# Turning the next group's x by DMA instead of on TensorE, and one attention chunk a unit earlier, in a fused local-attention and FFN kernel

## The chip, the cores and the metric

The kernel runs on one core of one Trainium2 chip. Its time is device microseconds of one execution; the time before is the median of three runs, 606.39 us (605.71, 606.39 and 606.4). One further execution was profiled, and all rows of the trace come from it. TensorE's granted clock was 1.0 throughout.

## The reference

The input x is 1 x 2048 x 640, float32. Two branches read the same layer-normalized x, and their product is added to x:

```python
xn = layernorm(x)
qkv = (xn @ wqkv).reshape(B, S, 3, H, Dh)          # 32 heads of 20
idx = pos[:, None] - (arange(8) * 2)[None, :]      # 8 keys, every second token back
logits = einsum("bhsd,bhswd->bhsw", q, k[idx]) * scale   # masked where idx < 0
s = (softmax(logits) with v[idx]).reshape(B, S, D) @ wo
g = silu(silu(xn @ w1) @ w2)                       # w1 640x1536, w2 1536x640
return x + s * g
```

## The kernel before, in words

**Groups.** The 2048 tokens are worked on in four groups of 512: two halves of the sequence, in each the even and then the odd tokens. A group is T = 4 tiles of 128 partitions by 640 columns. The 640 columns are DC = 5 chunks of 128; the 1536 hidden columns are FC = 12 units of 128.

**Products.** A float32 product is made of three matmuls of type float32r: high part by high part, low by high, high by low. So each operand exists as a high and a low half. For the operand that comes from x, TensorE needs columns on partitions: `split_t` turns one chunk. It makes four 128x128 transposes on TensorE (L619) into one of two PSUM banks named rot, ScalarE copies the bank to the high half TH (L623), and VectorE subtracts to the low half TL (L629). For x, ScalarE also copies the turned chunk back into XIN (L625, the buffer of normalized x), so that the subtraction (L626) reads it from there and the bank is free sooner. The turned chunk of attention's output O goes through the same function with L619, L623 and L629, into the halves OH and OL, which share buffers with TH and TL in alternation. Weights stand in a ring WR of seven tiles. At first use ScalarE (L564) and VectorE or GpSimd (L568) split them and SP stores the halves in DRAM (L573); later uses load both halves with one DMA from GpSimd's queue (L555).

**Stages of a group.** `qkv_phase` makes q, k and v (L886 to L888), ScalarE moves them out of PSUM (L641, L643), SP shifts rows between partitions for the window (L654, and L662 to L666 for the two rows carried from the first half of the sequence), and attention runs on VectorE, with an exp on ScalarE at L700 and some adds on GpSimd. It is not finished when the FFN starts: VectorE works at it beside the FFN's matmuls. `ffn_phase` is a list of steps on TensorE (`plan`):

- w1 unit 0, then `wo_phase`, which applies wo to the attention of the group before. VectorE multiplies the result into the gate tile G (L965); for each of the four tiles SP loads x again into one of three buffers xr (L978), GpSimd adds G to it (L979), and SP stores the output (L981).
- then w1 units and w2 units in the order of `STEPS`. A w1 unit (`up`, L1065 to L1067) is 15 matmuls into one rot bank, after which ScalarE writes silu twice, sh and sf (L1078, L1079), and VectorE their difference sl (L1080). A w2 unit (`down`, L930 and L932) is 24 pairs of matmuls with sh and sl, into the six acc banks.
- behind some w2 units, given by the table `AFTER`, the turn of one chunk of the next group's x. That x was loaded (L1010 is used for the last group) and normalized in XIN at the start of the FFN. In the last group there is no next x; there `AFTER` places the first three chunks of the last attention's output (`o_chunk`).
- at the end ScalarE writes silu of the acc banks into G (L1136).

In the last group the two remaining chunks of O are turned by `o_rest` (L779, then L782 and L783), the first two tiles ahead of the last w1 unit and the other two in the midst of it, after `at` chunks of its five. Then `wo_rest` adds the outputs of the third group, and `wo_last` applies wo to the last group. `first_quarter` holds the start of the program.

**Order.** Each engine runs its instructions in order, and each queue of DMAs starts them in order. All steps are put on a list with an engine, an assumed duration, the keys that they read and write, and a priority. The class `Weave` replays that list in a model of time. The order of TensorE is the order of the program; on the other engines the step that can start soonest goes first, by priority among equals. DMAs have an assumed rate and landing time (`RATE`, `LAND`, `more`), `at` holds a step back to a point in the model's time (`clock[0]` is TensorE's place), `late` delays its reader, and `lock` marks steps of VectorE and GpSimd that exclude one another. Where the model shows a gap on TensorE, `plan` tries other orders. `emit` then writes the instructions in the order found. So an edit of one table can move instructions on all engines.

Of the kernel before, what the change touches and what calls it, by code (L numbers as in the profile page):

```python
# [7 lines left out]

F32 = mybir.dt.float32
F32R = mybir.dt.float32r  # L10
AF = mybir.ActivationFunctionType
OP = mybir.AluOpType
AX = mybir.AxisListType

P = 128
# [36 lines left out]
OUT_IN = 6.0  # L52
CARRY_AT = 8.0
X_SINGLE = (1,2,)
QAT = 48
OAT = 16
STORE_Q = 1, 3
# [257 lines left out]
def local_attention_silu_ffn(ctx: ExitStack, tc: tile.TileContext, x, wqkv, wo, w1, w2, out):  # L315
# [11 lines left out]
    AFTER = ({1: 0, 3: 1, 5: 2, 7: 3, 9: 4}, {1: 0, 3: 1, 5: 2, 7: 3, 9: 4}, {1: 0, 3: 1, 5: 2, 7: 3, 9: 4}, {5: 0, 7: 1, 9: 2})  # L327
    STEPS = [
# [45 lines left out]
    XR = tiles("xr", 3, [P, D])  # L374
    SF = sb.tile([P, TOK], F32, name="sf")
    MARK = small("mark", 1)
    ACC = [psum.tile([P, TOK], F32, name=f"acc{i}") for i in range(6)]
    ROT = [psum.tile([P, TOK], F32, name=f"rot{i}") for i in range(2)]
    carry = [dram.tile([2, NQ, 2, T, CQ], F32, name=f"carry{par}") for par in range(2)]
# [251 lines left out]

    def tile_spans(of, cs, ts):
        return [(of, t * D + c * P, t * D + (c + 1) * P, False) for t in ts for c in cs]
# [417 lines left out]
    def up(g, i, f, io):  # L1054

        wh, wl, kh, kl = w_next("w1", f)
        h, kp = rot()
        s = f % NS

        def first(cs):  # L1060
            to = h.rearrange("p (m h) -> p m h", h=2)
            for c in cs:
                cs = tsl(c)
                hi, lo = (two(v[i][:, c, :], 0, TOK, TOK // 2) for v in (TH, TL))
                nc.tensor.matmul(to, wh[:, cs], hi, start=c == 0, stop=False)  # L1065
                nc.tensor.matmul(to, wh[:, cs], lo, start=False, stop=False)  # L1066
                nc.tensor.matmul(to, wl[:, cs], hi, start=False, stop=c == DC - 1)  # L1067
        at = 2 if g == NG - 1 and f == FC - 1 else DC
        for a, b in ((0, at), (at, DC)):
            if a == b:  # L1070
                continue
            if a:
                o_rest(g, (2, 3), io)
                wo_rest(g - 1, io)
            pe(3 * (b - a) * mm(TOK), lambda a=a, b=b: first(range(a, b)), t_keys(i, range(DC)) + [kh, kl], [kp])
        w_done()
        sh, sl = SH[s], SL[s]
        act(TOK, lambda: nc.scalar.activation(halves_of(sh), paired(h), AF.Silu), [kp], [("sh", s)], 0, "silu")  # L1078
        act(TOK, lambda: nc.scalar.activation(halves_of(SF), paired(h), AF.Silu), [kp], ["sf"], 0, "silu")  # L1079
        dve(TOK, lambda: nc.vector.tensor_tensor(out=sl, in0=SF, in1=sh.bitcast(F32), op=OP.subtract),  # L1080
            [("sh", s), "sf"], [("sl", s)], 0, lock=True)
# [24 lines left out]
    def ffn_phase(g, i, ix, io):  # L1106
        if g + 1 < NG:
# [7 lines left out]
            for t in range(T):  # L1115
                ln_apply(t)
        ps = None
        for kind, f in plan(g):
            if kind == "w1":
                up(g, i, f, io)  # L1120
            elif kind == "wo":
                wo_phase(g - 1, io)
                if g == NG - 1:
                    free_for([("xin", t) for t in range(T)], [("xin", t, c) for t in range(T) for c in (0, CA)])
            elif kind == "x":
                split_t(XIN, [("xin", t) for t in range(T)], f, ix, (TH, TL), XIN[:, :, tsl(f)])
            elif kind == "o":
                o_chunk(g, f, io)
            elif kind == "rest":
                o_rest(g, f, io)  # L1130
# [46 lines left out]
```

## Time and profile before

| | before |
|---|---|
| median of three runs | 606.39 us |
| profiled execution | 605.28 us |
| span in its trace | 603.5 us |
| busiest engine | TensorE, 597.0 us in 3495 matmuls |
| next | VectorE 518.4, ScalarE 222.2, GpSimd 165.7 us |
| bytes moved by DMA | 160.80 MB, 266 GB/s over the span |

Rows of the trace are read as follows. In a timeline and in the chain a row has the start in us from the span's start, the duration in us, the engine, and the source line with the operation; "out<-in" are the program's names of the buffers, then shapes and a count; brackets at the end give the idle time before the row and what ended it. PEld is TensorE's loading of weights, SPq and POOLq are DMAs that SP and GpSimd issue. In the table of groups the columns behind the bar are total busy time (us), mean of one (ns), and the idle time before.

The FFN of the second group lies at about 189 to 286 us of the span, that of the third at 337 to 434 us; the last w1 unit of the fourth group begins at about 571 us.

### The profile page before, as it was taken

The numbers are of one execution on the slowest core, as the hardware profiler recorded it, in microseconds if no ns is written. First come the engines' busy times: TensorE is split into PE (matmuls) and PEld (weight loads), VectorE is DVE, ScalarE is ACT, GpSimd is POOL, SyncE is SP. The second block draws the span as 40 slices with busy tenths as digits, with TensorE's granted clock in tenths as the row PEclk, the third lists the DMA queues.
The fourth block names the chain that finished last, engine by engine and source line by source line (L and its number), as shares of the span: only waits on it lengthen the run. The fifth ranks groups of instructions, "written<-read, shape, count | busy, mean of one in ns | idle before, by whom it ended". The sixth has DMA issues, their size and how long they took to land.

```text
span 603.5 us, 9128 instructions
## 1 busy us (share of the span) xinstructions
PE 597.0 (99%) x3495; PEld 562.0 (93%) x3495; DVE 518.4 (86%) x505; ACT 222.2 (37%) x426; POOL 165.7 (27%) x229
## 2 busy tenths in 40 slices
PE   8999999999999999999999999999999999999997
PEld 7999999999999999999999999999999999999897
DVE  6599999999799969999969999999727999998534
ACT  5447364453436124333324522242512341314220
POOL 5800111233110254343210126433122233531100
PEclk9999999999999999999999999999999999999999
DMA  9999999779999998655699998866789997766642
GB/s 294 308 321 323 330 407 394 285 244 303 284 323 293 320 318 250 205 169 163 185 320 285 328 348 289 273 210 178 226 220 274 301 324 259 249 186 210 209 163 87
DMA packets 66119, 160.80 MB, mean 266 GB/s; under 512 B 5805, under 2 KB 30093, under 8 KB 66077
## 3 DMA queue, kind: packets, MB, share of 16 engines
q0 software_dynamic: 19296, 79.31, 43.4%
q1 hardware_dynamic: 46237, 80.52, 43.0%
q8 instruction: 27, 0.44, 0.3%
q10 hardware_dynamic: 544, 0.41, 0.2%
q14 instruction: 15, 0.12, 0.1%
HBM read 107.91 MB, written 34.16 MB: 235 GB/s over the span
## 4 chain that ended last, share of the span: by engine, by line
PE 98%; DVE 1%; DMA 1%; ACT 0%; issue 0%
PE acc L930 22%; PE acc L932 15%; PE acc L886 10%; PE acc L887 10%; PE acc L888 10%; PE rot L1065 9%; PE rot L1067 9%; PE rot L1066 9%; PE rot L619 2%; PE acc L836 2%; DMA xin<-in_A_x_dram 1%; PE rot L820 0%; PE rot L1048 0%; DVE st L805 0%; DVE tl L629 0%; ACT th L623 0%
## 5 line engine op out<-in xcount | busy, mean ns | idle before, releaser
L680 DVE TENSOR_TENSOR pr<-q,kv 128x2560 f32<-128x2560 f32 x32 | 91.9, 2873 | 22.0 <-DMA kv<-kv 17.6
L886 PE MATMUL acc<-w,th 128*128 128x480 f32 x300 | 110.8, 369 | 0.0
L887 PE MATMUL acc<-w,tl 128*128 128x480 f32 x300 | 109.8, 366 | 0.0
L888 PE MATMUL acc<-w,th 128*128 128x480 f32 x300 | 109.8, 366 | 0.0
L930 PE MATMUL acc<-w,sh 128*128 128x384 f32 x384 | 109.1, 330 | 0.0
L932 PE MATMUL acc<-w,sh 128*128 128x256 f32 x384 | 104.7, 273 | 0.0
L1065 PE MATMUL rot<-th,w 128*128 128x512 f32 x240 | 92.2, 384 | 1.0 <-DVE tl L629 1.0
L722 DVE TENSOR_TENSOR pr<-q,kv 128x2560 f32<-128x2560 f32 x32 | 90.3, 2820 | 0.9
L1066 PE MATMUL rot<-tl,w 128*128 128x512 f32 x240 | 91.0, 379 | 0.0
L1067 PE MATMUL rot<-th,w 128*128 128x512 f32 x240 | 91.0, 379 | 0.0
L683 DVE TENSOR_REDUCE l<-pr 128x128 f32<-128x2560 f32 x32 | 89.6, 2799 | 0.2
L555 POOL DMA_DIRECT2D w<-half_w x72 | 39.0, 542 | 153.8 <-PE rot L1067 51.0
L932 PEld LDWEIGHTS acc<-w,sh 128*128 128x128 f32 x384 | 73.7, 192 | 0.6
L930 PEld LDWEIGHTS acc<-w,sh 128*128 128x128 f32 x384 | 72.6, 189 | 0.6
L1078 ACT ACTIVATE sh<-rot 128x512 fp32r<-128x512 f32 x48 | 28.8, 599 | 113.9 <-PE rot L1067 113.9
L555 POOL DMA_DIRECT2D w<-half_q x52 | 27.9, 537 | 122.6 <-PE acc L888 75.4
L888 PEld LDWEIGHTS acc<-w,th 128*128 128x128 f32 x300 | 56.7, 189 | 4.0
L887 PEld LDWEIGHTS acc<-w,tl 128*128 128x128 f32 x300 | 56.7, 189 | 3.8
L886 PEld LDWEIGHTS acc<-w,th 128*128 128x128 f32 x300 | 56.7, 189 | 3.8
L930 PE MATMUL acc<-w,sl 128*128 128x384 f32 x192 | 55.9, 328 | 0.0
L623 ACT ACTIVATE th<-rot 128x512 fp32r<-128x512 f32 x33 | 19.8, 600 | 89.9 <-PE rot L619 89.9
L932 PE MATMUL acc<-w,sl 128*128 128x256 f32 x192 | 52.3, 273 | 0.0
(101 smaller groups left out, 1079.4 us busy)
## 6 DMA issues: line engine op xcount, KB each, us to landing
w<-half_w POOLq DMA_DIRECT2D x72, 640.0 KB, 5.1
w<-half_q POOLq DMA_DIRECT2D x52, 480.0 KB, 5.8
half_w<-w SPq DMA_DIRECT2D x24, 640.0 KB
half_q<-w SPq DMA_DIRECT2D x20, 480.0 KB
kv<-kv SPq DMA_DIRECT2D x15, 560.0 KB
w<-half_wo POOLq DMA_DIRECT2D x10, 640.0 KB, 5.9
kv<-kv SPq DMA_DIRECT2D x15, 420.0 KB
gate<-in_B_w_dram SPq DMA_DIRECT2D x16, 320.0 KB
```

Of the source, the lines that this page charges most:

```text
L555: add("POOL", 1.0, lambda: nc.gpsimd.dma_start(both, src), [("half", u)], [kh, kl], due + 10, nbytes=2 * n * P * 4)
L680: dve(2560, lambda: nc.vector.tensor_tensor(out=PR, in0=win(qq[:, t:t + 2, :], W, 0), in1=win(kv[:, 0, t:t + 2, :], W, CQ), op=OP.mult), h ...
L683: dve(2560, lambda: nc.vector.tensor_reduce(out=l[:, t:t + 2].rearrange("p t w h -> p (t w h)"), in_=PR.rearrange("p t w (h d) -> p (t w h ...
L722: dve(2560, lambda: nc.vector.tensor_tensor(out=PR.rearrange("p t w (h d) -> p t (w h) d", d=DH), in0=e[:, t:t + 2].rearrange("p t w h -> ...
L886: nc.tensor.matmul(o, hi, vh, start=c == 0, stop=False)
L887: nc.tensor.matmul(o, lo, vh, start=False, stop=False)
L888: nc.tensor.matmul(o, hi, vl, start=False, stop=c == DC - 1)
L930: nc.tensor.matmul(a[t][0][:, :CA].rearrange("p (m h) -> p m h", h=2), st, col_a(w), start=first, stop=last)
L932: nc.tensor.matmul(b[t // 2][0][:, h * CB:(h + 1) * CB].rearrange("p (m h) -> p m h", h=2), st, col_b(w), start=first and h == 0, stop=las ...
L1065: nc.tensor.matmul(to, wh[:, cs], hi, start=c == 0, stop=False)
L1066: nc.tensor.matmul(to, wh[:, cs], lo, start=False, stop=False)
L1067: nc.tensor.matmul(to, wl[:, cs], hi, start=False, stop=c == DC - 1)
```

## The change

Three things are changed.

**Eight chunks of the next x are turned by DMA.** These are all five of the third group's x, in the second group's FFN, and the last three of the fourth group's x, in the third group's FFN. The dictionary `X_DMA` says which. DMA transposes 16-bit elements here, so the new function `turn_x` takes a float32 chunk as two planes of 16 bits. ScalarE copies the chunk apart into two planes (1024 elements of 16 bits a partition, L656) in a staging buffer. SP issues one transposing DMA per plane (L660, 128 partitions by 4 x 128 elements). ScalarE puts the planes together again, turned, into XIN (L665), and copies the high half (L670); VectorE subtracts for the low half (L671). No transposes on TensorE and no rot bank are used for these chunks.

The staging buffers are a new tile TURN and pieces of the gate tile G, 512 elements wide. G is in use until GpSimd's adds of `wo_phase` have read it, so the copies wait for the adds that cover the piece (`free_for`), and the silu at the end of the FFN (L1136 before, L1183 after), which writes G anew, waits for the pieces to be read. `PACE0`, `PACE` and `BACK` set when the copies may start in the model; `ISSUE` and `SLOW` are its assumptions on the DMA's issue and landing.

**The last attention's third chunk** goes from behind w2 unit 9 to behind unit 8 (`AFTER[3]`).

**The second `o_rest`** stands after three chunks of the last w1 unit rather than two (`at`).

The diff, cut to its core:

```diff
 X_SINGLE = (1,2,)
+X_DMA = {1: (0, 1, 2, 3, 4), 2: (2, 3, 4)}
+X_BY = {1: 2, 3: 0, 4: 1}
+SLOW, ISSUE, SUB_LATE = 8, 2.0, 3
+PACE0, PACE = -20.0, 12.0
+BACK = {1: 0.0, 2: 40.0}
...
-    AFTER = (..., {5: 0, 7: 1, 9: 2})
+    AFTER = (..., {5: 0, 7: 1, 8: 2})
...
+    TURN = sb.tile([P, TOK], F32, name="turn")
...
+    def turn_x(c, i, at, back):
+        keys = [("xin", t) for t in range(T)]
+        (a, ka), (b, kb) = (piece(G, X_BY[c]), ("buf", X_BY[c])) if c in X_BY else (TURN, ("turn",)), (piece(G, c), ("buf", c))
+        into = XIN[:, :, c * P:(c + 1) * P]
+        act(2 * TOK, lambda: nc.scalar.activation(
+            a.bitcast(U16).rearrange("p (h t n) -> p h t n", h=2, t=T), into.bitcast(U16).rearrange("p t (n h) -> p h t n", h=2),
+            AF.Copy), keys, both(ka), 150, at=at, spans=chunk_span("x", c))
+        for h in range(2):
+            dma(lambda h=h: nc.sync.dma_start_transpose(
+                b.bitcast(U16).rearrange("p (h t n) -> p h t n", h=2, t=T)[:, h],
+                a.bitcast(U16).rearrange("p (h n) -> p h n", h=2)[:, h]),
+                [ka + (h,)], [kb + (h,)], P * TOK * 6, clock[0], ISSUE, SLOW)
+        kh, kl = t_keys(i, [c], kinds=["th"]), t_keys(i, [c], kinds=["tl"])
+        act(2 * TOK, lambda: nc.scalar.activation(
+            into.bitcast(U16).rearrange("p t (n h) -> p h t n", h=2),
+            b.bitcast(U16).rearrange("p (h t n) -> p h t n", h=2, t=T), AF.Copy),
+            both(kb) + keys, [("xw", c)], 150, more=0.3, at=back, spans=chunk_span("x", c, True))
+        hi, lo = (v[i][:, c, :].rearrange("p (t n) -> p t n", t=T) for v in (TH, TL))
+        act(TOK, lambda: nc.scalar.activation(hi, into, AF.Copy), [("xw", c)] + keys, kh, 0)
+        dve(TOK, lambda: nc.vector.tensor_tensor(out=lo, in0=into, in1=hi.bitcast(F32), op=OP.subtract),
+            [("xw", c)] + keys + kh, kl, 0, lock=True, late=SUB_LATE, spans=chunk_span("x", c))
...
-        at = 2 if g == NG - 1 and f == FC - 1 else DC
+        at = 3 if g == NG - 1 and f == FC - 1 else DC
...
+                for c in range(DC) if by_dma else ():
+                    ts = slice(c * TOK // D, ((c + 1) * TOK - 1) // D + 1)
+                    free_for(gkeys(ts, slice(0, CA)) + gkeys(ts, slice(CA, D)), bufs[2 * c:2 * c + 2])
+                for k, c in enumerate(by_dma):
+                    turn_x(c, ix, clock[0] + PACE0 + PACE * k, clock[0] + BACK[g])
             elif kind == "x":
-                split_t(XIN, [("xin", t) for t in range(T)], f, ix, (TH, TL), XIN[:, :, tsl(f)])
+                if f not in by_dma:
+                    split_t(XIN, [("xin", t) for t in range(T)], f, ix, (TH, TL), XIN[:, :, tsl(f)])
...
-            act(n, lambda p=p, ts=ts, cs=cs: nc.scalar.activation(gate(ts, cs), p, AF.Silu), [kp], gkeys(ts, cs), 0, "silu")
+            act(n, lambda p=p, ts=ts, cs=cs: nc.scalar.activation(gate(ts, cs), p, AF.Silu), [kp], gkeys(ts, cs) + bufs * bool(by_dma), 0, "silu")
```

The inserted lines shift the numbers of the lines below them: `split_t` is L626 to L636 after, attention's exp L739, `o_rest` L818 to L822, the w2 matmuls L969 and L971, the output's load, add and store L1017, L1018 and L1020, the w1 matmuls L1104 to L1106, its silu L1117 and L1118, the weight loads L562 and L535 for their raw form.

On SP's queue in the second group's FFN there stand, before, the output's loads (L978) and stores (L981), raw weights of wo (L528), and the carried rows of the next group (L664):

```order
L978 DMA xr_109<-in_A_x_dram 128x640
L981 DMA out_dram<-xr_107 128x640
L981 DMA out_dram<-xr_108 128x640
L981 DMA out_dram<-xr_109 128x640
L978 DMA xr_107<-in_A_x_dram 128x640
L528 DMA xr_108<-in_A_wo_dram 128x640
L528 DMA xr_109<-in_A_wo_dram 128x640
L981 DMA out_dram<-xr_107 128x640
L528 DMA xr_107<-in_A_wo_dram 128x640
L664 DMA kv_93<-carry_120 1x2x640
```

On the same queue after the change:

```order
L1017 DMA xr_109<-in_A_x_dram 128x640
L1020 DMA out_dram<-xr_107 128x640
L1020 DMA out_dram<-xr_108 128x640
L660 DMA_TRANSPOSE gate<-turn 128x4x128 x2
L1017 DMA xr_107<-in_A_x_dram 128x640
L660 DMA_TRANSPOSE gate<-gate 128x4x128 x2
L1020 DMA out_dram<-xr_109 128x640
L535 DMA xr_108<-in_A_wo_dram 128x640
L535 DMA xr_109<-in_A_wo_dram 128x640
L1020 DMA out_dram<-xr_107 128x640
L535 DMA xr_107<-in_A_wo_dram 128x640
L660 DMA_TRANSPOSE gate<-turn 128x4x128 x2
```

The first four transposes stand among the output's loads and stores; four more (gate<-gate) follow the last row shown, and then the carried rows.

On ScalarE in the second group's FFN, between attention's exp (a table load and q<-l) and the silu of w1 unit 6 (a table load and sh), there stand before:

```order
L700 ACTIVATE q_98<-l_104 128x4x64
L623 ACTIVATE th_67<-rot_119 128x512
L625 ACTIVATE xin<-rot_119 128x4x128
L623 ACTIVATE th_67<-rot_118 128x512
L625 ACTIVATE xin<-rot_118 128x4x128
L1078 ACT_TABLE_LOAD
L1078 ACTIVATE sh_84<-rot_119 128x512
```

At the same place after the change:

```order
L739 ACTIVATE q_98<-l_104 128x4x64
L665 ACTIVATE xin<-gate 128x2x4x128
L670 ACTIVATE th_67<-xin 128x512
L656 ACTIVATE turn<-xin 128x1024
L656 ACTIVATE gate<-xin 128x1024
L665 ACTIVATE xin<-gate 128x2x4x128
L670 ACTIVATE th_67<-xin 128x512
L656 ACTIVATE gate<-xin 128x1024
L1117 ACT_TABLE_LOAD
L1117 ACTIVATE sh_84<-rot_119 128x512
```

Four short copies became seven, of which five are of 1024 16-bit elements. L665 waits for the transposes, L656 for the piece of G or TURN that it writes.

On ScalarE in the third group's FFN, at w1 unit 2, one of the copies stands after the change between the two silu outputs of one unit, where sh and sf stood in a row before:

```order
L1117 ACTIVATE sh_86<-rot_120 128x512
L656 ACTIVATE gate<-xin 128x1024
L1118 ACTIVATE sf<-rot_120 128x512
L656 ACTIVATE gate<-xin 128x1024
L739 ACT_TABLE_LOAD
L739 ACTIVATE q_98<-l_104 128x4x64
```

On TensorE in the last group, from the end of w2 unit 9 into the last w1 unit (rot1 and rot0 are the two rot banks), there stand before:

```order
L932 MATMUL acc3_115<-w5_80,sl0_87 128x256
L619 MATMUL rot1_119<-ident_65,o_101 128x128 x4
L779 MATMUL rot0_118<-ident_65,o_101 128x128 x4
L1065 MATMUL rot1_119<-th1_70,w6_81 128x512
L1066 MATMUL rot1_119<-tl1_74,w6_81 128x512
L1067 MATMUL rot1_119<-th1_70,w6_81 128x512
L1065 MATMUL rot1_119<-th1_70,w6_81 128x512
L1066 MATMUL rot1_119<-tl1_74,w6_81 128x512
L1067 MATMUL rot1_119<-th1_70,w6_81 128x512
L779 MATMUL rot0_118<-ident_65,o_101 128x128 x4
```

And after the change:

```order
L971 MATMUL acc3_116<-w5_80,sl0_87 128x256
L818 MATMUL rot0_119<-ident_65,o_101 128x128 x4
L1104 MATMUL rot1_120<-th1_70,w6_81 128x512
L1105 MATMUL rot1_120<-tl1_74,w6_81 128x512
L1106 MATMUL rot1_120<-th1_70,w6_81 128x512
L1104 MATMUL rot1_120<-th1_70,w6_81 128x512
L1105 MATMUL rot1_120<-tl1_74,w6_81 128x512
L1106 MATMUL rot1_120<-th1_70,w6_81 128x512
L1104 MATMUL rot1_120<-th1_70,w6_81 128x512
L1105 MATMUL rot1_120<-tl1_74,w6_81 128x512
L1106 MATMUL rot1_120<-th1_70,w6_81 128x512
L818 MATMUL rot0_119<-ident_65,o_101 128x128 x4
```

The turn that filled rot1 directly ahead of the last w1 unit is gone from this place, and nine matmuls instead of six lie between the two turns of `o_rest` that share rot0.

More of the change, by code (lines that the diff above doesn't have):

```diff
@@ L10 @@
 F32R = mybir.dt.float32r
+U16 = mybir.dt.uint16
 AF = mybir.ActivationFunctionType
@@ L326, in local_attention_silu_ffn @@
     og = out.rearrange("b (g p j) d -> (b g) p j d", p=P, j=J)
-    AFTER = ({1: 0, 3: 1, 5: 2, 7: 3, 9: 4}, {1: 0, 3: 1, 5: 2, 7: 3, 9: 4}, {1: 0, 3: 1, 5: 2, 7: 3, 9: 4}, {5: 0, 7: 1, 9: 2})
+    AFTER = ({1: 0, 3: 1, 5: 2, 7: 3, 9: 4}, {1: 0, 3: 1, 5: 2, 7: 3, 9: 4}, {1: 0, 3: 1, 5: 2, 7: 3, 9: 4}, {5: 0, 7: 1, 8: 2})
     STEPS = [
@@ L630, in split_t, with both, chunk_span, piece @@
             [kp] + kh, kl, 0)
+    def both(k):
+        return [k + (0,), k + (1,)]
+    def chunk_span(of, c, write=False):
+        return [(of, c * P, (T - 1) * D + (c + 1) * P, write)]
+    def piece(tile_of, k):
+        return tile_of.rearrange("p t d -> p (t d)")[:, k * TOK:(k + 1) * TOK]
+    def turn_x(c, i, at, back):
[19 more added lines that the diff above has]
+            [("xw", c)] + keys + kh, kl, 0, lock=True, late=SUB_LATE, spans=chunk_span("x", c))
     def tile_spans(of, cs, ts):
@@ L1117, in ffn_phase @@
         ps = None
+        by_dma = X_DMA.get(g, ())
+        bufs = [("buf", c, h) for c in range(DC) for h in range(2)]
         for kind, f in plan(g):
```

## Prediction

> **What bounds the kernel now.** I read the page's busy shares first, then the chain that ended last, then the waits of TensorE.
>
> ```profile
> PE 597.0 (99%) x3495; PEld 562.0 (93%) x3495; DVE 518.4 (86%) x505; ACT 222.2 (37%) x426; POOL 165.7 (27%) x229
> PE 98%; DVE 1%; DMA 1%; ACT 0%; issue 0%
> PE rot L792 <- POOL ident masks.py:199: 1.4, 1, 1.4
> PE rot L1065 <- DVE tl L629: 1.0, 1, 1.0
> PE rot L820 <- DVE xin L810: 0.2, 1, 0.2
> ```
>
> The first line gives busy time per engine, the second the chain by engine, the last three every wait of TensorE (total, times, longest). TensorE is busy or on the chain 98% of the span, and once the first microseconds are over it waits exactly once, for 1.0 us. So whatever TensorE no longer has to do shortens the kernel one for one, unless one of the new steps makes it wait. The profiled execution took 605.28 us (span 603.5); the median of the runs is 606.39 us, 1.1 us more. I make the sum against 605.28 and carry the difference to the median.
>
> **Removed: eight turns on TensorE.** The chain in order of time (start, length, what) shows each turn of a 128-column chunk of x. These are the first and last of the five in the second group's FFN and of the three in the third's that go, and the matmul behind the first.
>
> ```profile
> 222.18 0.44 PE rot L619 x4
> 225.91 0.22 PE rot L1065
> 279.38 0.44 PE rot L619 x4
> 393.69 0.44 PE rot L619 x4
> 427.14 0.44 PE rot L619 x4
> ```
>
> Four transposes take 0.44 us, and work stands directly before and after them. 8 x 0.44 = 3.52 us leave a chain that has no gaps. The same rows give one w2 unit: 225.91 - 222.62 = 3.29 us.
>
> **Moved: the last attention's third chunk.** The one wait of 1.0 us is at this place (TensorE's timeline, and the chain's steps for the same stretch).
>
> ```profile
> 571.06 0.60 PE L779 MATMUL rot<-ident,o 128*128 128x128 f32 x4
> 572.64 0.48 PE L1065 MATMUL rot<-th,w 128*128 128x512 f32 x1 [0.98 <-DVE tl L629]
> 570.79 0.45 PE rot L619 x4
> 571.26 0.61 ACT th L623
> 571.89 0.70 DVE tl L629
> 547.89 0.49 DVE L735 TENSOR_TENSOR o<-pr 128x320 f32<-128x320 f32 x1
> ```
>
> The turn fills one of two rot banks, the next turn the other, and the last w1 unit wants the first bank back: turn start to next matmul takes 572.64 - 570.79 = 1.85 us, of which 572.64 - 571.06 - 0.44 = 1.1 us is empty. With the chunk one unit earlier, the last w1 unit finds its bank long free. The chunk's input is ready in time: its last write is the 547.89 row, and the new place is about 564. What is late next is the second o_rest turn, which needs the first one's bank: 1.85 us after the first began. Behind the first now stand nine matmuls instead of six, 0.44 + 9 x 0.22 = 2.4 us, so nothing waits. Gain 1.1 us (0.98 by the wait's own row).
>
> **Added on ScalarE.** Each of the eight chunks gains two copies of 1024 16-bit elements (L656, L665) and keeps one of 512 (L670 for L623); the L625 copy goes. No row shows a strided 16-bit copy. Rows by size (count | busy, mean ns):
>
> ```profile
> L643 ACT ACTIVATE q<-acc 128x160 f32<-128x160 f32 x64 | 19.4, 305 | 0.0
> L623 ACT ACTIVATE th<-rot 128x512 fp32r<-128x512 f32 x33 | 19.8, 600 | 89.9 <-PE rot L619 89.9
> L564 ACT ACTIVATE w<-xr 128x640 fp32r<-128x640 f32 x18 | 13.0, 740 | 3.7 <-DMA xr<-in_A_wo_dram 3.5 <-DMA xr<-in_B_w_dram 0.2
> ```
>
> (740 - 305) / 480 = 0.91 ns an element, so 740 + 384 x 0.91 = 1.09 us is my estimate; the ends are the 0.74 of the 640-element row and twice my value. Net +1.6 us a chunk, 13 us on an engine that is idle 63% of the span. What counts is its order. The densest place is in the second group, where seven copies stand between an exp and the w1 unit 6 silu:
>
> ```profile
> 238.06 0.42 ACT L700 ACTIVATE q<-l 128x256 f32<-128x256 f32 x1
> 247.50 1.28 ACT L1078 ACT_TABLE_LOAD   x1
> 249.64 0.60 ACT L1078 ACTIVATE sh<-rot 128x512 fp32r<-128x512 f32 x1 [0.85 <-PE rot L1067]
> ```
>
> One turn less before it, the exp ends at 238.04. Five long copies (5.45) and two short (1.2) end at 244.7, the table load at 246.0; the silu's matmul ends at 249.64 - 3 x 0.44 = 248.3. So 2.3 us are spare, and TensorE itself only notices when unit 8 wants unit 6's bank, a unit (15 x 0.22 = 3.3 us) later: 5.6 us over five copies. They hide up to 2.2 us each, which is the upper end. Cost nothing.
>
> **Added on the SP queue and the DMA engines.** 16 transposing DMAs of 128 KB. No row shows one. The nearest are the halo copies from SBUF to SBUF: their issue (min/median/max ns), and in the fourth group their landing.
>
> ```profile
> L654 SPq DMA_DIRECT2D kv<-kv x68: 544/864/1972, 22.2 to 488.2; - x68
> 446.81 3.57 SPq L654 DMA_DIRECT2D kv<-kv  x5
> 456.94 2.82 DVE L680 TENSOR_TENSOR pr<-q,kv 128x2560 f32<-128x2560 f32 x1 [16.09 <-DMA kv<-kv]
> 243.29 0.63 SPq L664 DMA_DIRECT2D kv<-carry  x1
> 311.79 2.83 DVE L680 TENSOR_TENSOR pr<-q,kv 128x2560 f32<-128x2560 f32 x1 [4.15 <-DMA xin<-in_A_x_dram]
> ```
>
> Issue 0.5 to 2.0 us, landing up to 456.94 - 446.81 = 10.1 us; I take the upper ends of both, because a block turn can hardly be cheaper than a copy. The tightest chain is chunks two to four of the second group: six issues in a row from about 240.7, when the first of their copies is written. The last lands at 240.7 + 6 x 2.0 + 10.1 = 262.8. Its reader, chunk four's L665, stands on ScalarE behind w1 unit 10's sf. Here are that sf, the like for the third group, three weight loads of POOL, their landing (KB each, us), and the two stretches of the second group's FFN, whose last two numbers are DMA share and GB/s:
>
> ```profile
> 273.39 0.59 ACT L1079 ACTIVATE sf<-rot 128x512 f32<-128x512 f32 x1
> 404.37 0.59 ACT L1079 ACTIVATE sf<-rot 128x512 f32<-128x512 f32 x1
> 383.69 0.53 POOL L555 DMA_DIRECT2D w<-half_w  x1 [1.16 <-PE rot L1067]
> 232.68 0.57 POOL L555 DMA_DIRECT2D w<-half_w  x1 [0.32 <-PE rot L1067]
> 235.93 0.53 POOL L555 DMA_DIRECT2D w<-half_w  x1 [2.67 <-PE rot L1067]
> w<-half_w POOLq DMA_DIRECT2D x72, 640.0 KB, 5.1
> 209.00:245.00 36.00, 36.00 (x224) 33.99 (x223) 29.99 (x23) 9.35 (x16) 18.89 (x21) 1.00 0.85 266
> 245.00:286.00 41.00, 41.00 (x252) 38.59 (x252) 40.10 (x30) 16.02 (x26) 14.71 (x21) 1.00 0.59 176
> ```
>
> That is 273.98 - 4 x 0.44 = 272.2, 9.4 us after the landing. TensorE would only miss unit 11's silu at w2 unit 11: the next group begins at 279.82 + 2 x 3.29 - 2.2 = 284.2, the unit at 280.9, less 2.2 for ScalarE's three steps: 278.7. So six issues and a landing may take 38 us together; I expect 22. In the third group the last four issues follow POOL's fourth add, which now stands behind the load of the 383.69 row: 383.7 - 2.2 + 0.5 + 1.6 = 383.6, and with 4 x 2.0 + 10.1 they land at 401.7; their readers stand behind unit 8's sf, 404.96 - 2.6 = 402.3, and TensorE would miss the silu behind them only at w2 unit 9 (427.14 - 3.29 - 3.1 = 420.8), less 4.0 for ScalarE: 33 us for 18. Queued behind the transposes on SP are a residual load, two stores, three weight loads and the carry load of the 243.29 row; that one, some 10 us later now, is read by the next group's first score, which starts at 311.79. Weight loads on POOL share the DMA engines: one a unit (235.93 - 232.68 = 3.25 us), into a ring of seven, so each has 6 x 3.25 - 5.1 = 14 us to spare. Cost nothing.
>
> The Trainium skill speaks against this change: VectorE: DVE Perf Modes, "The three transpose paths" and the rules behind it, prices a 128x128 block at 1309 ns by DMA against 390 ns on TensorE and advises TensorE where PSUM will do as the destination. By its figure a plane of four blocks is 5.2 us (an estimate), six are 31 us: the chain would end near 274, still before TensorE misses it, and the sum would stay. The 0.44 us for four turns in the chain's rows is cheaper on TensorE than the page has it; TensorE just happens to be the engine with no idle time.
>
> **Sum.** 3.52 + 1.1 = 4.6 us: 605.28 - 4.6 = 600.7 for a profiled execution, 606.39 - 4.6 = 601.8 for the median. That is my forecast, chance 0.74.
>
> **Rival: part is given back in the third group** (0.10). ScalarE's copy of chunk three now stands between sh and sf of w1 unit 2 and waits for POOL's add of the first gate tile:
>
> ```profile
> 363.89 0.59 ACT L1079 ACTIVATE sf<-rot 128x512 f32<-128x512 f32 x1
> 364.46 1.54 POOL L979 TENSOR_TENSOR xr<-xr,gate 128x640 f32<-128x640 f32 x1 [0.26 <-DMA xr<-in_A_x_dram]
> 388.55 0.68 DVE L1080 TENSOR_TENSOR sl<-sf,sh 128x512 fp32r<-128x512 f32 x1
> 386.67 0.44 PE rot L619 x4
> ```
>
> The add ends at 366.0, the copy at 367.1, sf starts 3.2 us later than before, and VectorE, in order, waits with its sl. The sl of unit 5 (ends 389.2) is wanted at 387.11 + 3.29 + 2/3 x 3.29 = 392.6: 3.4 us spare against 3.2 lost, so a little more contention makes TensorE wait, 1 to 3 us: 602.8 to 604.8. Against it: VectorE meets 16.09 us of idle time at the next group (row above), so nothing lasts.
>
> **Rival: the turns fill the DMA engines** (0.10), ending slower. The two stretches above moved 266 and 176 GB/s; the page's best slice moved 407:
>
> ```profile
> GB/s 294 308 321 323 330 407 394 285 244 303 284 323 293 320 318 250 205 169 163 185 320 285 328 348 289 273 210 178 226 220 274 301 324 259 249 186 210 209 163 87
> ```
>
> Free are 36 x (1 - 266/407) + 41 x (1 - 176/407) = 36 us for ten planes, and the ring absorbs 14 us: TensorE waits for weights once a plane holds the engines for over (36 + 14) / 10 = 5.0 us, and the gain is gone at 5.5. At 6 us it would lose 10 us: 612. The nearest row speaks against it, 560 KB in 10.1 us being 2.4 us for 128 KB. By the Trainium skill's 1309 ns (the section named above), if a block did keep all engines, 10 x 5.2 = 52 us would cost 2 us: 604; the same skill's Advanced Engine Details and Errata, "X-Bar Transpose (TRN2)", has these DMAs as fast as others, which costs nothing; no row here decides between them.
>
> **Rival: no net change** (0.06), within 0.2% (1.2 us, about what a measurement of this kernel can tell): another engine's order paces the FFN and the turns only filled its wait. Against it stands the list of waits: TensorE has none there, so 605.2 to 607.6 needs a new stall of 3.4 to 5.8 us. That the turns stay is excluded by the order of TensorE: it has seven turns of x on this line where there were fifteen.
>
> **Chances.** Faster: 0.74 + 0.10 = 0.84; same 0.06; slower 0.10. The range takes the forecast less the 1.1 us between median and profiled run below, 600.7, and reaches above to the end of the partial case, 604.8; no change and slower, 0.16 together, stay out.
>
> **What would show it.** In the profile after: L626 with 25 turns instead of 33 (eight less), no wait on the last w1 unit, and TensorE's busy time 3.5 us shorter with no wait above 0.5 us. ScalarE's L656 and L665 near 1.1 us. Transposes issued in at most 2 us and landed within 12. A wait of TensorE on sf, sl or w in the second or third group's FFN would be the first or second rival; a time above 604.8 refutes the sum.

## The result, and the profile after

The change takes the kernel from 605.71 to 601.3 us (medians of five runs each, 605.2 to 606.4 and 600.52 to 602.59). The ratio is 0.9927, with a 95% interval of 0.9915 to 0.994: 4.4 us less, where 4.6 was forecast. The profiled execution went from 605.28 to 600.52 us, 4.8 less; 600.7 was forecast for it.

The page of the kernel after: span, busy times, and the chain by engine.

```profile
span 598.7 us, 9085 instructions
...
PE 593.2 (99%) x3463; PEld 558.4 (93%) x3463; DVE 515.6 (86%) x505; ACT 236.9 (40%) x434; POOL 163.5 (27%) x229
...
PE 98%; DMA 1%; DVE 0%; issue 0%
```

And the whole list of what TensorE waited for (total, times, longest):

```profile
PE rot L831 <- POOL ident masks.py:199: 1.4, 1, 1.4
PE rot L859 <- DVE xin L849: 0.2, 1, 0.2
```

TensorE has 32 matmuls fewer (eight turns of four transposes) and is busy 3.8 us less; the wait of 1.0 us on the last w1 unit is gone and none has come in its place. 3.8 + 1.0 is the whole 4.8. ScalarE is busy 14.7 us more, and TensorE waits for none of it.

The last group's tail in TensorE's timeline: the two turns of `o_rest`, and the matmul behind each.

```profile
567.54 0.60 PE L818 MATMUL rot<-ident,o 128*128 128x128 f32 x4
567.90 0.46 PE L1104 MATMUL rot<-th,w 128*128 128x512 f32 x1
...
569.92 0.60 PE L818 MATMUL rot<-ident,o 128*128 128x128 f32 x4
570.28 0.46 PE L1104 MATMUL rot<-th,w 128*128 128x512 f32 x1
```

No row has an idle time in brackets: the last w1 unit follows the first turn at once, and the second turn comes 2.38 us after the first, later than the bank needs.

The new groups on ScalarE (busy, mean ns), and the transposing DMAs (issue in ns, min/median/max; then the time from issue to landing):

```profile
L665 ACT ACTIVATE xin<-gate 128x1024 uint16<-128x1024 uint16 x8 | 10.9, 1366 | 0.0
...
L656 ACT ACTIVATE gate<-xin 128x1024 uint16<-128x1024 uint16 x5 | 5.2, 1050 | 2.7 <-POOL xr L1018 2.7
L670 ACT ACTIVATE th<-xin 128x512 fp32r<-128x512 f32 x8 | 5.1, 632 | 0.3
...
L656 ACT ACTIVATE turn<-xin 128x1024 uint16<-128x1024 uint16 x3 | 3.1, 1046 | 0.0
```

```profile
L660 SPq DMA_TRANSPOSE gate<-gate x10: 1212/1303/1564, 219.1 to 389.5; - x10
...
L660 SPq DMA_TRANSPOSE gate<-turn x6: 1202/1438/1930, 215.2 to 367.6; - x6
...
DMA to landing us min/median/max: 6.0/7.2/8.5
```

The copy apart takes 1.05 us (estimate 1.09), the copy back 1.37; issues stay under the 2.0 us and landings under the 10.1 us that the prediction took as upper ends.

### The profile page after: what moved, and what is told of

The parts are those of the page before. It is cut to its first block, busy times and chain, and to the rows that moved or that the text cites. A ratio compares the mean times of both kernels' runs of the same rounds, so it can differ in the third digit from the quotient of the medians.

```text
span 598.7 us, 9085 instructions
## 1 busy us (share of the span) xinstructions
PE 593.2 (99%) x3463; PEld 558.4 (93%) x3463; DVE 515.6 (86%) x505; ACT 236.9 (40%) x434; POOL 163.5 (27%) x229
## 4 chain that ended last, share of the span: by engine, by line
PE 98%; DMA 1%; DVE 0%; issue 0%
PE acc L969 22%; PE acc L971 15%; PE acc L925 10%; PE acc L926 10%; PE acc L927 10%; PE rot L1104 9%; PE rot L1106 9%; PE rot L1105 9%; PE acc L875 2%; PE rot L626 2%; DMA xin<-in_A_x_dram 1%; PE rot L859 0%; PE rot L1087 0%; DVE st L844 0%; PE rot L818 0%; DVE gate L1055 0%
## 5 line engine op out<-in xcount | busy, mean ns | idle before, releaser
L969 PE MATMUL acc<-w,sh 128*128 128x384 f32 x384 | 108.6, 328 | 0.0
L971 PE MATMUL acc<-w,sh 128*128 128x256 f32 x384 | 104.7, 273 | 0.0
L1104 PE MATMUL rot<-th,w 128*128 128x512 f32 x240 | 92.1, 384 | 0.0
L1106 PE MATMUL rot<-th,w 128*128 128x512 f32 x240 | 91.0, 379 | 0.0
L1117 ACT ACTIVATE sh<-rot 128x512 fp32r<-128x512 f32 x48 | 28.8, 599 | 138.5 <-PE rot L1106 138.4
L562 POOL DMA_DIRECT2D w<-half_w x72 | 38.8, 539 | 156.5 <-PE acc L971 56.8
L971 PEld LDWEIGHTS acc<-w,sh 128*128 128x128 f32 x384 | 73.7, 192 | 0.6
L969 PEld LDWEIGHTS acc<-w,sh 128*128 128x128 f32 x384 | 72.6, 189 | 0.6
L562 POOL DMA_DIRECT2D w<-half_q x52 | 27.8, 535 | 122.9 <-PE acc L927 75.4
L969 PE MATMUL acc<-w,sl 128*128 128x384 f32 x192 | 55.9, 328 | 0.0
L1119 DVE TENSOR_TENSOR sl<-sf,sh 128x512 fp32r<-128x512 f32 x48 | 42.0, 876 | 14.3 <-ACT sf L1118 14.1
L971 PE MATMUL acc<-w,sl 128*128 128x256 f32 x192 | 52.3, 273 | 0.0
```

What stands on the lines that cost most here:

```text
L562: add("POOL", 1.0, lambda: nc.gpsimd.dma_start(both, src), [("half", u)], [kh, kl], due + 10, nbytes=2 * n * P * 4)
L969: nc.tensor.matmul(a[t][0][:, :CA].rearrange("p (m h) -> p m h", h=2), st, col_a(w), start=first, stop=last)
L971: nc.tensor.matmul(b[t // 2][0][:, h * CB:(h + 1) * CB].rearrange("p (m h) -> p m h", h=2), st, col_b(w), start=first and h == 0, stop=las ...
```

## The experiments

All ratios below are against the kernel before on the same chip.

### 1. The tail alone (e1)

```diff
-X_DMA = {1: (0, 1, 2, 3, 4), 2: (2, 3, 4)}
+X_DMA = {}
```

> The kernel after with no chunk turned by DMA: all fifteen turns of x stay on TensorE, and only the last attention's third chunk stands behind unit 8 and the second o_rest after three chunks. Theory (TensorE's own time and its one wait): TensorE loses nothing but the wait of 1.0 us on the last w1 unit, so 605.7 - 1.1 = 604.6 us, ratio 0.998, and the wait on VectorE's tl is gone from the list of TensorE's waits. Rival (the tail's wait only moves, to the second o_rest or to the acc banks): 605.7, with a wait of about 1 us elsewhere in the last group.

Measured: 604.38 us against 605.5, ratio 0.998 [0.9969, 0.9991], 1.1 us less, as the theory has it. Its profiled execution was one of the longer ones, 605.26 us, and shows why:

```profile
485.95 0.48 PE L1104 MATMUL rot<-th,w 128*128 128x512 f32 x1 [0.91 <-DVE tl L636]
```

This is w1 unit 0 of the same group, 85 us before the tail, where VectorE is late with the low half of an attention chunk, because a score before it waited for its halo copies:

```profile
473.37 2.83 DVE L719 TENSOR_TENSOR pr<-q,kv 128x2560 f32<-128x2560 f32 x1 [3.16 <-DMA kv<-kv]
```

The tail itself has no wait. A wait at this place, of 0.5 to 1.05 us, stands in the profiles of experiments 2, 3 and 11 too, and in those of before, after and experiment 9 it doesn't. That it comes and goes between executions of one kernel, as a part of the scatter of the runs, is likely but not shown: each kernel has one profile.

### 2. The DMA turns alone (e2)

```diff
-{5: 0, 7: 1, 8: 2}
+{5: 0, 7: 1, 9: 2}
...
-        at = 3 if g == NG - 1 and f == FC - 1 else DC
+        at = 2 if g == NG - 1 and f == FC - 1 else DC
```

> The eight chunks turned by DMA, with the last group's order as before (third chunk behind unit 9, second o_rest after two chunks). Theory: 8 x 0.44 = 3.5 us less, 605.7 - 3.5 = 602.2 us, and the wait of 1.0 us on VectorE's tl ahead of the last w1 unit is in the list again. Rival (the turns by DMA cost something that the tail's rearrangement pays back): over 603.0 us. Rival (the gain comes from the tail alone): 605.7.

Measured: 602.76 us, ratio 0.9948 [0.9935, 0.9962], by the ratio 3.1 us less. TensorE's waits in its profile (an execution of 603.18 us):

```profile
482.60 0.48 PE L1104 MATMUL rot<-th,w 128*128 128x512 f32 x1 [1.05 <-DVE tl L636]
570.55 0.48 PE L1104 MATMUL rot<-th,w 128*128 128x512 f32 x1 [0.97 <-DVE tl L636]
```

The second row is the tail's wait, back as expected; the first is at the place of experiment 1. Without it this execution would be 602.1 us, where 602.2 was expected. Tail and turns alone add up to 1.2 + 3.1 = 4.3 us by the ratios, and to 1.1 + 2.7 = 3.8 by the medians, of the 4.4 us.

### 3. The second group alone (e3)

```diff
-X_DMA = {1: (0, 1, 2, 3, 4), 2: (2, 3, 4)}
+X_DMA = {1: (0, 1, 2, 3, 4)}
```

> DMA turns in the second group's FFN alone (five chunks), the new tail kept. Theory: 5 x 0.44 + 1.1 = 3.3 us less than before, 602.4 us, 1.3 us more than the whole change. Rival (the third group gives part back): no slower than the whole change, 601.3 us or less. Rival (the second group's denser DMA traffic costs): over 603.0 us.

Measured: 602.33 us, ratio 0.9943 [0.9928, 0.9959]. That is the theory's 602.4; the third group's three turns are worth 1.0 us (expected 1.3) and give nothing back.

### 4. The turns put back on TensorE, unread (e4)

```diff
                 if f not in by_dma:
                     split_t(...)
+                else:
+                    spare, ks = rot()
+                    pe(0.44, lambda ...: [nc.tensor.transpose(spare[:, tsl(t)], ident, ident) for t in range(T)], [], [ks])
```

> The whole change, and beside it TensorE still makes eight turns at the old eight places, of the identity into a rot bank, which nobody reads. All DMA turns and ScalarE copies stay. Theory (TensorE has no idle time there, its time counts one for one): 601.3 + 8 x 0.44 = 604.8 us. Rival (the turns only filled waits, and the gain came from ScalarE and VectorE no longer reading the rot banks, or from the new order): 601.3 to 602 us.

Measured: 604.9 us, ratio 0.9988 [0.9976, 1.0]: 3.6 us more than the change, 0.45 us a turn. TensorE is busy 596.9 us again, against 593.2. The profile also has one wait in the FFNs, so up to 0.5 of the difference may be that:

```profile
401.36 0.48 PE L1104 MATMUL rot<-th,w 128*128 128x512 f32 x1 [0.50 <-ACT sf L1118]
```

All DMAs and ScalarE's copies are still there, so TensorE's own time is what the turns by DMA save, and the rest of them costs nothing.

### 5 and 6. Every transposing DMA twice, and four times (e5, e6)

```diff
-            dma(lambda h=h: nc.sync.dma_start_transpose(...),
+            dma(lambda h=h: [nc.sync.dma_start_transpose(...) for _ in range(2)],   # e6: range(4)
```

> The whole change, with every transposing DMA issued twice into the same place (32 of them instead of 16), the order otherwise the same. The profile of after shows an issue of about 1.45 us, a landing of 6.0 to 8.5, and some 1.5 us of all sixteen engines for a plane (the queues' shares, before against after). Theory (hidden with room to spare): twelve issues and a landing are 12 x 1.45 + 8.5 = 26 us of the 38 that the prediction allowed, two times 1.5 us a plane stay under its 5.0, so 601.3 us and no new wait of TensorE. Rival (the DMA turns are just covered, any more shows): 16 x 1.45 us of SP or more of the engines, 602.5 us and up.

> As the one before, with every transposing DMA issued four times (64). Theory: both bounds of the prediction are passed. 24 issues and a landing are 24 x 1.45 + 8.5 = 43 us against 38, and four times 1.5 = 6.0 us a plane against 5.0; TensorE waits for sf behind the late L665 or for weights, 5 to 10 us: 606 to 612 us. Rival (weight loads and halos don't share anything with the transposes): 601.3 to 602.

Measured: 633.22 us (ratio 1.0447 [1.0425, 1.0468]) and 717.1 us (1.1828 [1.179, 1.1865]). The theory is far off in both, and the rival's 602.5 and up names no such size. The experiment did not do what it was meant to: the second DMA writes where the first did, so it waits on SP for the first's landing. SP's queue in e5's second group, six pairs:

```profile
255.18 13.29 SPq L660 DMA_TRANSPOSE gate<-turn  x4
268.57 20.77 SPq L660 DMA_TRANSPOSE gate<-gate  x8
```

34 us for what took 8.7 us in after. The longest waits of TensorE in e5 (in e6 the same three take 72.7, 3.6 and 21.8 us), and ScalarE's copy of chunk four in e5:

```profile
PE rot L1104 <- ACT sf L1118: 12.7, 3, 5.8
PE acc L969 <- DVE sl L1119: 3.8, 2, 2.7
PE acc L969 <- ACT sh L1117: 3.6, 1, 3.6
```

```profile
292.36 1.34 ACT L665 ACTIVATE xin<-gate 128x1024 uint16<-128x1024 uint16 x1 [7.88 <-DMA gate<-gate]
...
294.26 0.58 ACT L1117 ACTIVATE sh<-rot 128x512 fp32r<-128x512 f32 x1
```

So the two runs show the other half of the prediction's step on SP: a late landing holds ScalarE at L665, the silu behind it in ScalarE's order comes late, and TensorE waits for sh and sf. The prediction had 278.7 us as the latest start for chunk four; in after it is 272.09, here 292.36. They say nothing on how much load the DMA engines bear; experiments 8 to 12 are about that.

### 7. ScalarE's long copies twice (e7)

```diff
-        act(2 * TOK, lambda: nc.scalar.activation(...), ...)           # L656 and L665
+        act(2 * TOK, lambda: [nc.scalar.activation(...) for _ in range(2)], ...)
```

> The whole change, with ScalarE's two copies of 1024 elements (L656 and L665) made twice each, in the same order. In after they take 1.05 and 1.37 us. Theory (spare of 5.6 us at the densest place of the second group): three and two copies there take 3 x 1.05 + 2 x 1.37 = 5.9 us more, 0.3 over the spare, and in the third group sf of w1 unit 2 comes another 1.05 us later where the prediction had 0.2 us of room: 0.3 to 1.5 us in all, 601.6 to 602.8 us, the wait being one for sf, sh or sl. Rival (ScalarE is idle 60% of the span and so it costs nothing): 601.3 us, no wait. Rival (the copies lie on the path): 8 x 2.4 = 19 us, 620.

Measured: 604.29 us, ratio 0.9982 [0.9965, 0.9999], 3 us more than the change and above the 602.8 us expected at most; the nine executions took 602.73 to 606.62. The profiled one took 603.12, 2.6 more than that of the change: TensorE is busy 0.8 us more (594.0 against 593.2) and has one new wait, shown here with two rows of ScalarE:

```profile
253.46 0.48 PE L1104 MATMUL rot<-th,w 128*128 128x512 f32 x1 [1.74 <-ACT sf L1118]
```

```profile
252.32 0.60 ACT L1117 ACTIVATE sh<-rot 128x512 fp32r<-128x512 f32 x1
252.82 0.59 ACT L1118 ACTIVATE sf<-rot 128x512 f32<-128x512 f32 x1
```

The wait stands where the theory put it, at unit 8 of the second group, which wants the bank that sf of unit 6 reads. It is longer than the 0.3 us expected there, because the bank is free only when sf ends: 252.82 + 0.59 - 252.32 = 1.1 us after sh begins. The prediction counted its spare to sh. So 2.3 + 3.3 - 1.1 = 4.5 us are to be had, not 5.6, and 5.9 more should cost 1.4 us; the row has 1.74. What the executions of 604.9 us and more waited for, no profile shows. ScalarE, idle 60% of the span, does have a place where 5 us count.

### 8. All five chunks of the third group too (e8)

```diff
-X_DMA = {1: (0, 1, 2, 3, 4), 2: (2, 3, 4)}
+X_DMA = {1: (0, 1, 2, 3, 4), 2: (0, 1, 2, 3, 4)}
```

> DMA turns for all five chunks in the third group's FFN as well (ten chunks in all). Theory: two more turns of 0.44 us leave TensorE, 601.3 - 0.9 = 600.4 us. Rival (the first two chunks come too late there, since VectorE and ScalarE are behind with attention when G's first pieces come free, so that TensorE waits for sf, sl or for th of the next group): 601.3 to 603 us with such a wait in the list.

Measured: the median is 606.06 us, but the executions fall in two clumps, five of twelve at 599.86 to 601.29 us and seven at 605.74 to 610.7. The lower clump is the theory's 600.4. The profiled execution is of the upper one, 608.7 us, and waits for neither sf, sl nor th:

```profile
397.61 0.79 PE L1104 MATMUL rot<-th,w 128*128 128x512 f32 x1 [7.14 <-DMA w<-half_w]
```

The landing of weight loads (us from issue, the loads issued from 365 to 412 us, in the third group's FFN) in this execution:

```profile
DMA to landing us min/median/max: 5.7/17.7/24.6
```

The same for before, and for after:

```profile
DMA to landing us min/median/max: 4.1/5.4/10.1
```

```profile
DMA to landing us min/median/max: 4.1/6.9/14.7
```

The load that TensorE waited for, with the time from its issue to its landing; the issue of the gate<-gate transposes in the third group (ns, min/median/max); and the landing of weight loads in the second group of the same execution (205 to 260 us):

```profile
374.13 1.10 POOL L562 DMA_DIRECT2D w<-half_w  x2
DMA to landing us min/median/max: 23.4/23.4/23.4
L660 SPq DMA_TRANSPOSE gate<-gate x6: 1197/1478/8500, 368.9 to 414.7; - x6
DMA to landing us min/median/max: 4.1/6.2/9.9
```

So the rival that the prediction held for unlikely, turns that crowd the DMA engines until TensorE waits for weights (a choke, from here on), is real; one chunk more than the change doesn't show it (experiment 9), two more do. The waited-for load was issued at 374.13 and would have been wanted at 397.61 - 7.14 = 390.47, so a load at this place had 16.3 us from issue to need. The prediction's sum has 6 x 3.25 = 19.5, of which it counted 14 as delay that the ring bears beyond the usual landing of 5.1; here it is 11. The expectation of experiment 9, which puts a landing of 24.6 us against "the ring's 14", compares a landing with a delay: the landing has to be held against the 16.3, or at most the 19.5, us. The longest landing after the change, 14.7 us, is already near that.

### 9. Four chunks (e9)

```diff
-X_DMA = {1: (0, 1, 2, 3, 4), 2: (2, 3, 4)}
+X_DMA = {1: (0, 1, 2, 3, 4), 2: (1, 2, 3, 4)}
```

> DMA turns for four chunks in the third group's FFN (all but the first) beside the second group's five. SP's queue here has the fourth residual load ahead of all transposes of the third group. Theory (what choked the run with five chunks were two pairs of transposes close behind each other amid stores and loads, so that weight loads landed after up to 24.6 us, more than the ring's 14; one turn fewer on TensorE is worth its 0.44 us): 601.3 - 0.4 = 600.9 us, longest landing of a weight load in the third group at most 15 us, no wait of TensorE for w. Rival (it is the number of planes in the third group, 6 in the change, 8 here, 10 there): 603 to 606 us, a wait for w of some 3 us in part of the runs.

Measured: 600.05 us, 599.83 to 600.3 in four runs, ratio 0.9903 [0.9887, 0.9919]: faster than before and, by the medians, 1.25 us faster than the change, though the change's interval, 0.9915 to 0.994, overlaps it and one turn is worth only 0.44 us. Weight loads, same stretch:

```profile
DMA to landing us min/median/max: 4.1/7.4/11.9
```

No choke with eight planes, and TensorE's list has only the waits of the program's start.

### 10. Five chunks, the residual load ahead (e10)

```diff
 # order on SP's queue, third group
 L660 DMA_TRANSPOSE gate<-turn 128x4x128 x2
 L1020 DMA out_dram<-xr_107 128x640
+L1017 DMA xr_108<-in_A_x_dram 128x640
 L660 DMA_TRANSPOSE gate<-gate 128x4x128 x2
-L1017 DMA xr_108<-in_A_x_dram 128x640
```

> DMA turns for all five chunks in the third group's FFN as in the run that was slow, with one swap on SP's queue: the fourth residual load stands ahead of the second pair of transposes instead of behind it, so that the pair starts some 8 us later. Theory (the two pairs close together choke the weight loads): the choke goes, two turns fewer are worth 0.9 us: 600.4 us in all runs, longest landing of a weight load about 15 us. Rival (ten planes are too many wherever they stand): 606 us and a wait of TensorE for w as before.

Measured: four of six executions at 609.75 to 610.78 us, two at 600.0 and 602.31. The theory falls: the place of the load does not cure it. (One of twelve executions of the kernel before on this chip took 610.23 us too, so a single long one would say little; four of six do.) The profile is of the 600.0 us execution, with weight loads landing after up to 17.2 us and no wait for them; that the long ones waited for weights is argued from experiment 8.

### 11. Second `o_rest` after two chunks (e11)

```diff
-        at = 3 if g == NG - 1 and f == FC - 1 else DC
+        at = 2 if g == NG - 1 and f == FC - 1 else DC
```

> The whole change, with the second o_rest after two chunks of the last w1 unit as before; nothing else moves. Theory (second term of the sum: the second turn needs the bank of the first, 1.85 us after the first began; six matmuls fill 0.44 + 6 x 0.22 = 1.76 us): a wait of about 0.1 us at the second o_rest, 601.4 us, so all of the tail's 1.1 us is due to the chunk and not to the place of the second o_rest. Rival (the place of the second o_rest carries part of it): a wait of 0.5 us or more there, 601.8 us and up.

Measured: 602.11 us, ratio 0.994 [0.9925, 0.9954]. In its profile:

```profile
568.72 0.60 PE L818 MATMUL rot<-ident,o 128*128 128x128 f32 x4
...
570.73 0.66 PE L818 MATMUL rot<-ident,o 128*128 128x128 f32 x4
```

The second turn comes 2.01 us after the first. In after a turn and nine matmuls fill 569.92 - 567.54 = 2.38 us, so a turn and six fill 2.38 - 3 x 0.22 = 1.72: 0.3 us of stall, between the expectations. The median's 0.8 us over the change holds the wait at the place of experiment 1 besides (0.5 us in this profile), and the intervals overlap. The move to three chunks is worth some 0.3 us once the chunk stands earlier; that is a part of the tail's 1.1.

### 12. Plain copies in the place of transposes (e12)

```diff
 # on the kernel of experiment 8
-            dma(lambda h=h: nc.sync.dma_start_transpose(
+            dma(lambda h=h: nc.sync.dma_start(
```

> DMA turns for all five chunks in the third group's FFN, in the order of the run that was slow, but every transposing DMA is a plain copy of the same plane from the same buffer to the same buffer (the blocks are not turned, so x enters the next group unturned; all else is computed). Theory (a transposing DMA holds the DMA engines some 1.5 us for a plane of 128 KB, and that delays the weight loads to landings of up to 24.6 us): a plain copy moves 128 KB in 0.3 us at the 407 GB/s of the best slice, so no choke: 600.4 us in all runs, longest landing of a weight load in the third group at most 12 us, DMA share there back near 0.8. Rival (the choke comes from the order on SP's queue, from more issues, or from more bytes): 606 us in most runs, with a wait for w, as with the transposes.

This kernel leaves the turn out, so x is wrong in these ten chunks; the work of all engines stays. Measured: 600.04 us, 599.46 to 600.45 in four runs, ratio 0.9902 [0.9885, 0.9918]; no wait for w, and weight loads as in before:

```profile
DMA to landing us min/median/max: 4.1/5.3/8.6
```

Same order, same number of issues, same bytes: what chokes the weight loads is that the DMAs transpose. (At experiment 8's rate of seven in twelve, four executions without a choke would have a chance of (5/12)^4, 3%; the landings point the same way.) How much they take, the queues' shares say: for before (603.5 us), for this kernel (598.7), for the execution of experiment 10 that has twenty transposes instead (598.2), and for the choked one of experiment 8 (606.9):

```profile
q1 hardware_dynamic: 46237, 80.52, 43.0%
q1 hardware_dynamic: 49117, 83.14, 44.7%
q0 software_dynamic: 19296, 79.31, 43.2%
```

```profile
q1 hardware_dynamic: 57117, 83.15, 47.8%
q0 software_dynamic: 19296, 79.31, 45.4%
q1 hardware_dynamic: 57117, 83.15, 50.2%
```

q1 is SP's queue, q0 GpSimd's weight loads. Twenty transposes take 0.478 x 598.2 - 0.430 x 603.5 = 26.4 us of all sixteen engines, 1.3 us each; twenty copies take 18.3 us less, with 400 packets less each. In the choked execution it is 45.2 us, 2.3 each: the time of a packet grows with the crowding, so neither is a fixed price. The weight loads, the same in number and bytes, take 13 us more beside the transposes than beside the copies.

And one stretch of the third group's FFN in after (its first two transposes were issued at 366 to 369 us), and the same in this kernel; the last two numbers are DMA share and GB/s:

```profile
372.00:376.00 4.00, 4.00 (x20) 3.52 (x19) 3.90 (x4) 1.08 (x2) 2.40 (x4) 1.00 1.32 73
372.00:376.00 4.00, 4.00 (x21) 3.49 (x20) 3.97 (x5) 1.13 (x3) 3.50 (x5) 1.00 1.10 397
```

In this slice, behind the transposes, the engines are busy and move little by this view: 73 GB/s against 397 beside the copies.

## Why the prediction was right, point by point

**Eight turns, 3.52 us.** Right: TensorE's busy time fell by 3.8 us, e4 puts 3.6 back, e2 takes 3.1 by its ratio.

**The tail, 1.1 us.** Right in size (e1). The reason was right for the most part: the chunk's earlier place frees the bank. For the second `o_rest` the prediction's own 1.85 us against 0.44 + 6 x 0.22 = 1.76 us of work leaves 0.1 us to be had from its new place; e11 shows about 0.3.

**ScalarE's copies, nothing.** The result was right; the estimate of 1.09 us was 1.05 and 1.37. In after's second group the last of the seven copies and the table load leave this:

```profile
244.72 1.28 ACT L1117 ACT_TABLE_LOAD   x1
248.30 0.60 ACT L1117 ACTIVATE sh<-rot 128x512 fp32r<-128x512 f32 x1 [2.29 <-PE rot L1106]
```

2.29 us idle, where 2.3 were forecast. That it agrees to a hundredth is luck: from start to start the five long copies took 5.7 us and the two short ones 1.1, where 5.45 and 1.2 were put in, and they began 0.13 us earlier. The bound above it was wrong by 1.1 us, as e7 showed: 4.5 us to spare, not 5.6.

**SP and landings, nothing.** Right. In the second group the six issues began at 240.91, where 240.7 was forecast, ended at 249.6 and landed well ahead of chunk four's L665 at 272.09, which stands behind sf and waits for no DMA. In the third group:

```profile
385.41 5.44 SPq L660 DMA_TRANSPOSE gate<-gate  x4
```

They were issued by 390.9; the first of their readers stands on ScalarE at 402.19 behind unit 8's sf. The 14 us of spare for a weight load was too much, as e8 shows (11 at the place measured there); the longest landing after the change, 14.7 us, used 9.6 of it and TensorE waited for no weights.

**The first rival, sf of unit 2 in the third group.** Its mechanism is there, its price is not:

```profile
363.12 1.06 ACT L656 ACTIVATE gate<-xin 128x1024 uint16<-128x1024 uint16 x1 [1.34 <-POOL xr L1018]
364.31 0.60 ACT L1118 ACTIVATE sf<-rot 128x512 f32<-128x512 f32 x1
```

The copy waits for the add, and sf starts at 364.31, 2.6 us later than before's 363.89 less the 2.2 us gained; 3.2 was the sum. TensorE lost nothing by it, in e7 neither.

**The second rival, turns that fill the DMA engines.** It didn't happen in the change, and e8 with e12 shows that it can. What failed is its threshold: 5.0 us a plane, from the mean free time of two stretches and the ring's spare. A plane took 1.3 us here, 2.3 in the choked execution, both far under that, and ten such planes already choke the third group in most executions of e8. The mean hides it; what counts is how far the landing of single weight loads stretches, against the ring. (Its 2.4 us for 128 KB of a halo copy is 10.1 x 128 / 560 = 2.3.) The truth lies between two pages of the Trainium skill. VectorE: DVE Perf Modes, "The three transpose paths", would give 5.2 us a plane (an estimate from its 1309 ns a block), much more than the shares show. Advanced Engine Details and Errata, "X-Bar Transpose (TRN2)", has such DMAs as fast as regular ones, and beside this kernel's other traffic e8 against e12 contradicts it: same bytes, 600.04 us with copies, 606.06 in the median with transposes.

What stays open: why five chunks choke in some executions and not in others, and why eight planes in the third group with the load ahead of all (e9) didn't in four runs while ten in e10 did. The number of planes alone, or how close they follow each other, can't be it: in e8 the second group has ten planes as well, the first four issued between 215.1 and 222 us and six from 240.8 on, and there no weight load took over 9.9 us to land. What differs in the third group, the traffic around the planes (before moved 266 GB/s from 209 to 245 us, and 297 in the same stretch of the third group, 357 to 393) or the place of each plane in it, these runs don't tell apart.

## What to carry to other kernels

Where one engine is on the chain 98% of the span, time taken off it counts one for one, and the work is to show for each new step whose order it stands in and when that engine is next waited for; count the spare to the end of the last reader of the buffer, not to its start. That the mean load leaves room does not show that work moved to DMA is hidden: look at the longest landing of the loads that share the engines, and at how many the ring can bear. One step further in the same direction can bring the choke that the first step didn't, so try both neighbours of a chosen split; here four chunks in the third group were, by the medians, better than three (600.05 against 601.3 us), and five were worse in seven of twelve executions.

## What the runs showed of the hardware

A transposing DMA of a 128x512 plane of 16 bits took 1.2 to 1.9 us to issue in after and landed after 6.0 to 8.5 us; in the choked execution of e8 one issue took 8.5 us. A plain copy of the same plane took this to issue (e12):

```profile
L660 SPq DMA_DIRECT2D gate<-gate x12: 464/566/743, 219.7 to 405.4; - x12
```

A 16-bit ScalarE copy of 1024 elements took 1.05 us reading with a stride and 1.37 us writing with one.

After a long wait TensorE ran slower for a while. In e8, around its 7.1 us wait (the columns end with the granted clock, DMA share and GB/s):

```profile
395.00:405.00 10.00, 7.39 (x27) 6.24 (x28) 1.16 (x1) 2.26 (x3) 1.85 (x2) 0.71 1.34 160
405.00:415.00 10.00, 10.00 (x64) 9.49 (x63) 9.89 (x10) 9.58 (x13) 4.91 (x8) 1.00 1.22 235
```

In e5, with the 20.1 us of waits shown there, TensorE's busy time was 603.9 us against 593.2 in after for the same matmuls, so long waits cost more than their own length.
